# A decode kernel's last three microseconds: result in 16 rows of 144 columns, other weight pieces, and one early read

## Chip, cores, metric

The program uses one core of a Trainium2 chip (trn2). Runs of different rounds were on different chips, so each ratio is taken against the kernel before of the same rounds. The metric is the device time of the program in microseconds (us). The profiled span is about 1.8 us shorter than the device time (before: 210.4 against 212.2). The engines are PE (TensorE), DVE (VectorE), ACT (ScalarE), POOL (GpSimd) and SP (SyncE, which issues the DMAs here).

## The reference, cut to what matters

```python
# B = 4 batch rows, D = 576; 32 query heads, 16 KV heads of 128; a window of 2048 keys; F = 4608
xn  = layernorm(x)
A   = attention(xn @ wq, k_cache[last 2048], v_cache[last 2048]) @ wo
h   = gelu(layernorm(xn) @ w1) ...          # one token: all shifted parts are zero, so x1 = xn
Bm  = xn + gelu(layernorm(xn) @ w3) @ w4    # w4: 4608 x 576
out = x + A + Bm                            # 4 x 576, bf16
```

The K and V windows and the weights are read once, 87 MB. The result is 4.6 KB.

## The kernel before

All of `x + xn + A + gelu(..) @ w4` is summed in PSUM by PE. The result has 4 rows of 576 columns; the sum is kept as 8 rows of 288: row (batch, half). To aim a half at its row, the stationary operand is shifted by one column inside a tile that is zero elsewhere.

```python
CW = D // 2                                   # 288 columns
W4_PIECES = [0, 10, NFH, NFH + 10, NFH + 14, NF - 2, NF]      # NF = 36, NFH = 18: 10, 8, 10, 4, 2, 2 rows

OR = 2 * B                                    # 8 rows of the sum
OW = OR + 2
gT = cleared([P, NF, OW], "gT")               # activations, every second column, else zero
acc = ps_acc.tile([P, CW], F32)

def acc_matmuls(terms):
    for i in range(2):
        for n, (lhsT, rhs) in enumerate(terms):
            to, q, start = (second[0], QD, second[1]) if second and n % 2 else (acc, 0, False)
            nc.tensor.matmul(out=to[q:q + OR, :], lhsT=lhsT[:, 1 - i:1 - i + OR],
                             rhs=rhs[:, i * CW:(i + 1) * CW], start=start, stop=False, ...)
# ... (attention over 16 KV heads, the MLP's first product: cut)
mlp_out(*pieces[0])            # rows 0-9 of w4, odd rows into a second sum, acc_odd, in other PE columns
o_turn(hl); o_sum(hl); o_spread(hl); o_pick(hl)       # last attention head
mlp_out(*pieces[1])
o_proj(hl)
mlp_out(*pieces[2])
mlp_out(*pieces[3])
second.clear()                 # from here on all rows go into acc, one after the other
odd = const.tile([OR, CW], F32)
nc.scalar.activation(out=odd[:], in_=acc_odd[QD:QD + OR, :], func=ACT.Copy)
for lo, hi in pieces[4:]:
    mlp_out(lo, hi)
fin = const.tile([OR, CW], out.dtype)
nc.vector.tensor_tensor(out=fin[:], in0=acc[0:OR, :], in1=odd[:], op=ALU.add)
nc.sync.dma_start(out=o2.rearrange("b (i n) -> (b i) n", i=2), in_=fin[:])
```

While `second` is set, a pair of rows of w4 goes to two groups of PE columns at once, so a pair takes the time of one matmul. A "piece" is one DMA of w4; its landing releases PE for its rows. One "row" of w4 here is one of 36 slices of 128 x 576 in SBUF.

Of the kernel before, what the change touches and what calls it, by code (L numbers as in the profile page):

```python
# [9 lines left out]
ALU = mybir.AluOpType  # L10
AX = mybir.AxisListType
BF16 = mybir.dt.bfloat16
F32 = mybir.dt.float32
# [9 lines left out]
def kernel(  # L23
# [14 lines left out]
    nc = tc.nc  # L38
    P = 128
    B, Sq, D = A_x.shape  # L40
# [8 lines left out]
    NF = F // P  # L49
    NFH = NF // 2  # L50
# [4 lines left out]
    NQD = P // QD  # L55
    NSL = 4
    SC = NC // NSL
    CW = D // 2
    NW = SC * QD
    assert NW == 512 and NSL * NJ == QD and NQ == 2 * NQD * NW and NFH == 18  # L60
    scale = float(Dh) ** -0.5
# [5 lines left out]
    o2 = out.flatten_outer_dims()  # L67
# [14 lines left out]
    const = ctx.enter_context(tc.tile_pool(name="const", bufs=1))  # L82
# [47 lines left out]
        nc.sync.dma_start(out=t[:, KJ * F:], in_=B_w3[KJ * P:D, :].rearrange("r (e f) -> (r e) f", e=2))  # L130
        w_tiles["w3"] = t

    W4_PIECES = [0, 10, NFH, NFH + 10, NFH + 14, NF - 2, NF]

    def load_w4():
        t = wp.tile([P, NF, D], BF16, tag="w", name="w4_sb")
        for lo, hi in zip(W4_PIECES, W4_PIECES[1:]):
            e = lo // NFH
# [8 lines left out]
    ident_f = ident_w[:, 0:P]  # L147
# [7 lines left out]
    def cleared(shape, name):  # L155
        t = const.tile(shape, BF16, name=name)
        flat = t[:] if len(shape) == 2 else t[:].rearrange("p a b -> p (a b)")
        flat = flat.bitcast(F32)
        nc.scalar.activation(out=flat, in_=zero[:].bitcast(F32).to_broadcast(list(flat.shape)), func=ACT.Copy)
        return t  # L160
# [2 lines left out]
    ln2T = cleared([P, KJ + 2, QD], "ln2T")  # L163
    ZP = (NSL - 1) * NJ
    qz = cleared([P, ZP + Hkv * 4 * P], "qz")
    OR = 2 * B
    OW = OR + 2
    gT = cleared([P, NF, OW], "gT")
    op = cleared([P, WOR, OW], "op")

    acc = ps_acc.tile([P, CW], F32)
    nc.vector.memset(acc[:], 0.0)
# [2 lines left out]
    second = []  # L175

    def acc_matmuls(terms):
        for i in range(2):
            for n, (lhsT, rhs) in enumerate(terms):
                to, q, start = (second[0], QD, second[1]) if second and n % 2 else (acc, 0, False)  # L180
                nc.tensor.matmul(out=to[q:q + OR, :], lhsT=lhsT[:, 1 - i:1 - i + OR],  # L181
                                 rhs=rhs[:, i * CW:(i + 1) * CW], start=start, stop=False, skip_group_check=True)
                if start:
                    second[1] = False
# [43 lines left out]
    for kb in range(NQD):  # L228
        nc.vector.tensor_copy(out=sel[:, :, :, kb, :],
                              in_=ident_bf[:].rearrange("p (ib i e) -> p ib e i", ib=2, e=2))  # L230
# [19 lines left out]
    with nc.allow_low_precision("zeros and ones"):  # L250
# [7 lines left out]
                          in_=sel_j[:].unsqueeze(1).to_broadcast([P, NG, NJ]))  # L258
# [7 lines left out]

    idz = const.tile([B, OW], F32)
    nc.gpsimd.memset(idz[:], 0.0)
    nc.gpsimd.tensor_copy(out=idz[:, 1:OR + 1:2], in_=ident_f[0:B, 0:B])
    xsum = xn_f  # L270
    nc.vector.tensor_tensor(out=xsum[:], in0=xn_f[:], in1=x_bf[:], op=ALU.add)
    acc_matmuls([(idz[:], xsum)])
    ln2_bf = part(D, B)
    layernorm(None, ln2_bf, xn_bf)
# [25 lines left out]
    for r in range(2):  # L300
        nc.vector.tensor_copy(out=q_bf[:, r],
                              in_=qT_ps[:, r].rearrange("p u (g x) -> p g u x", g=NQD)[:, :, :, 0:B])
# [101 lines left out]
    def o_sum(h):  # L404
        oT = st.pop(("oT", h))
        v = oT[:].rearrange("p s (g x) -> p (s g) x", g=NQD)[:, :, 0:NJ].rearrange("p g (b r) -> p b r g", r=rep)
        k = h % WOQ
        if k == 0:
            st["on"] = small.tile([P, WOH, B], BF16, tag="on", name="on")
        with nc.allow_low_precision("summed in float32"):  # L410
            nc.vector.reduce_sum(out=st["on"][:, k * rep:(k + 1) * rep, :].rearrange("p r b -> p b r"),  # L411
                                 in_=v, axis=AX.X)
# [12 lines left out]
    def o_pick(h):  # L425
        if h % WOQ < WOQ - 1:
            return
        R = st.pop("R")
        mk = small.tile([P, WOR, WOH, B], BF16, tag="mk")
        nc.vector.tensor_tensor(out=mk[:], in0=R[:],  # L430
                                in1=own[:].unsqueeze(1).unsqueeze(3).to_broadcast([P, WOR, WOH, B]), op=ALU.mult)
        with nc.allow_low_precision("one term is not zero"):
            nc.vector.reduce_sum(out=op[:, :, 1:OR + 1:2], in_=mk[:].rearrange("p i h b -> p i b h"), axis=AX.X)

    def o_proj(h):
        if h % WOQ < WOQ - 1:
            return
        for i in range(0, WOR, 2):
            acc_matmuls([(op[:, i + u, :], wo_tiles[h // WOQ][:, i + u, :]) for u in range(2)])

    G_CHUNKS = [(e, 4 * g, 4) for e in range(2) for g in range(NQD)] + [(e, 16, 2) for e in range(2)]
    xs = const.tile([P, NF, B], F32, name="g_x")
# [31 lines left out]
    def mlp_act():  # L474
        u = const.tile([P, NF, B], F32, name="g_u")
        nc.vector.tensor_tensor(out=u[:], in0=xs[:], in1=xs[:], op=ALU.mult)
        nc.vector.tensor_scalar(out=u[:], in0=u[:], scalar1=GELU_A, scalar2=1.0, op0=ALU.mult, op1=ALU.add)
        nc.vector.tensor_tensor(out=u[:], in0=u[:], in1=xs[:], op=ALU.mult)
        nc.scalar.activation(out=u[:], in_=u[:], func=ACT.Tanh, scale=GELU_C)
        nc.vector.tensor_scalar(out=u[:], in0=u[:], scalar1=0.5, scalar2=0.5, op0=ALU.mult, op1=ALU.add)  # L480
        nc.vector.tensor_tensor(out=gT[:, :, 1:OR + 1:2], in0=u[:], in1=xs[:], op=ALU.mult)

    def mlp_out(lo, hi):
        w4 = w_tiles["w4"]
        for i in range(lo, hi, 2):
            acc_matmuls([(gT[:, i + u, :], w4[:, i + u, :]) for u in range(2)])


    order = [("K", 0), ("K", 1), ("K", 2)]
# [24 lines left out]
    for t in range(Hkv):  # L514
        hm, hv, hf, hp = t - 1, t - 2, t - 3, t - 4
        for s in range(NSL):
            if s == NSL - 1 and hm >= 0:
                sm_turn(hm)
            n = t * NSL + s + 1
# [3 lines left out]
            if s == 0:  # L523
                if hm >= 0:
                    sm_max(hm)
                if hv >= 0:
                    sm_rec(hv)
                if hp >= 0:
                    o_pick(hp)
                if hf >= 0:  # L530
                    o_scale(hf)
                k_mask(t)
            elif s == 1 and hm >= 0:
                sm_maxT(hm)
            elif s == 2:
                if hm >= 0:
                    sm_sub(hm)
                    sm_exp(hm)
                if hf >= 0:
                    o_sum(hf)  # L540
            elif s == 3 and hm >= 0:
                sm_den(hm)
# [12 lines left out]
            if t == G_AT:  # L555
                if s < 3:
                    mlp_g(s)
                if s > 0:
                    mlp_turn(s - 1)
                if s == NSL - 1:  # L560
                    mlp_act()
# [27 lines left out]
    o_sum(hl - 1)  # L589
    pieces = list(zip(W4_PIECES, W4_PIECES[1:]))  # L590
    acc_odd = ps_acc.tile([P, CW], F32, tag="g", name="acc_odd")
    second += [acc_odd, True]
    mlp_out(*pieces[0])
    o_turn(hl)
    o_sum(hl)
    o_spread(hl)
    o_pick(hl)
# [4 lines that stand above are left out]
    second.clear()  # L602
    odd = const.tile([OR, CW], F32)
    nc.scalar.activation(out=odd[:], in_=acc_odd[QD:QD + OR, :], func=ACT.Copy)
    for lo, hi in pieces[4:]:
        mlp_out(lo, hi)

    fin = const.tile([OR, CW], out.dtype)
    nc.vector.tensor_tensor(out=fin[:], in0=acc[0:OR, :], in1=odd[:], op=ALU.add)
    nc.sync.dma_start(out=o2.rearrange("b (i n) -> (b i) n", i=2), in_=fin[:])  # L610


# [28 lines left out]
```

## Time and profile before

| | before |
|---|---|
| device time, median of 3 | 212.24 us (212.07 to 212.55) |
| span of the profiled run | 210.4 us |
| DMA queue q1 | 87.17 MB, 97.4% of 16 engines' span |
| PE busy | 71% |
| last piece of w4 seen by PE | 207.09 us |

From the page of the kernel before: first the DMA row of 40 slices (tenths busy) and the bandwidth, then the DMA queues (packets, MB, share), then the chain that ended last, by engine.

```profile
DMA  7999999999999999999999999999999999999991
...
q1 hardware_dynamic: 6640, 87.17, 97.4%
q8 instruction: 7, 0.11, 0.2%
...
DMA 69%; PE 19%; DVE 8%; issue 1%; ACT 1%; SPq 0%; DVEq 0%
```

The DMA engines are at least 90% busy from the second slice to the 39th. Shortening work under this load is not expected to shorten the kernel, unless it moves fewer bytes or lets a transfer start sooner. What is left is the tail after the last weights.

The tail, from the timeline of the kernel before (start us, duration us, engine, line, operation, count; in brackets the engine's idle time before it and what ended that):

```profile
204.27 0.28 PE L181 MATMUL acc<-w_sb,gT 128*8 128x288 bf16 x1 [1.17 <-DMA w_sb<-in_B_w_dram]
...
206.35 0.40 ACT L604 ACTIVATE odd<-acc_odd 8x288 f32<-8x288 f32 x1 [7.80 <-PE acc_odd L181]
206.39 1.35 PE L181 MATMUL acc<-w_sb,gT 128*8 128x288 bf16 x8
206.39 0.45 PEld L181 LDWEIGHTS <-gT 128*8 128x8 bf16 x4 [0.28 <-issue]
207.09 0.33 PEld L181 LDWEIGHTS <-gT 128*8 128x8 bf16 x3 [0.25 <-issue]
207.85 0.45 DVE L609 TENSOR_TENSOR fin<-acc,odd 8x288 bf16<-8x288 f32 x1 [5.95 <-PE acc L181]
208.32 0.37 SPq L610 DMA_DIRECT2D out_dram<-fin  x1
```

And the end of the chain of waits of the kernel before (start us, us, what):

```profile
184.90 22.15 DMA w_sb<-in_B_w_dram
207.05 0.04 issue
207.09 0.67 PE acc L181 x4
207.75 0.03 issue
207.78 0.02 DVEq L609
207.80 0.04 issue
207.85 0.45 DVE fin L609
```

Here PE waits for DMA: the weight loads (PEld) stand idle 0.25 us before the last piece, and the chain goes from the DMA to the last four matmuls. Between them and the final add stands `DVEq L609`, a semaphore wait of its own on DVE: the add has to wait for PE and for ACT, and one of the two waits became a separate instruction. After the page's chain come the result's DMA, and SP's closing waits, which are not counted as busy. In the trace's records the last of these waits is passed at 209.59, 1.27 us after the result's DMA instruction starts; the program's close then takes 0.83 us.

### The profile page before, as it was taken

How to read it: one execution, taken by the hardware profiler on the slowest of the kernel's cores; microseconds unless marked ns; L12 is line 12 of the kernel's file. 1: busy time of each engine (PE TensorE's matmuls, PEld its weight loads, DVE VectorE, ACT ScalarE, POOL GpSimd, SP SyncE). 2: the span in 40 equal slices, each digit the busy share in tenths (PEclk: the TensorE clock that was granted, in tenths of full speed). 3: DMA queues.
4: the chain of work that ended last, by engine and by line, in shares of the span. 5: the costliest groups of instructions: out<-in, count | busy, mean ns of one | idle time of the engine just before them, and what ended most of it. 6: DMA issues, size and time to landing. Idle time of an engine off the chain costs nothing.

```text
span 210.4 us, 2389 instructions
## 1 busy us (share of the span) xinstructions
PE 149.7 (71%) x941; PEld 63.7 (30%) x955; DVE 120.3 (57%) x216; ACT 33.9 (16%) x64; POOL 2.8 (1%) x15
## 2 busy tenths in 40 slices
PE   0396595769691008649899599977995976888974
PEld 0132232123240003214364144333532321443542
DVE  4831989474850082825806878985399274683220
ACT  7603101020210000202102121120111020202300
POOL 4010000000000000000000000000000000000000
PEclk9999579796997555957999969997998596999999
DMA  7999999999999999999999999999999999999991
GB/s 281 417 399 436 424 437 419 434 436 424 440 441 411 439 420 426 440 436 420 439 430 420 439 421 436 427 436 431 420 438 430 424 432 433 424 433 425 427 400 52
DMA packets 6659, 87.32 MB, mean 415 GB/s; under 512 B 748, under 2 KB 760, under 8 KB 1400
## 3 DMA queue, kind: packets, MB, share of 16 engines
q1 hardware_dynamic: 6640, 87.17, 97.4%
q8 instruction: 7, 0.11, 0.2%
q14 instruction: 4, 0.03, 0.0%
q10 hardware_dynamic: 8, 0.00, 0.0%
HBM read 87.17 MB, written 0.00 MB: 414 GB/s over the span
## 4 chain that ended last, share of the span: by engine, by line
DMA 69%; PE 19%; DVE 8%; issue 1%; ACT 1%; SPq 0%; DVEq 0%
DMA vn<-in_A_v_cache_dram 37%; DMA w_sb<-in_B_w_dram 27%; PE S L336 7%; DMA wq_sb<-in_A_wq_dram 6%; DVE kt L223 4%; PE acc L181 2%; PE g_ps L454 2%; PE O L388 2%; PE q_ps L283 2%; PE oT L401 1%; DVE mx L342 1%; PE S L358 1%; DVE qz L315 1%; PE gT_ps L466 1%; PE qT_ps L298 0%
## 5 line engine op out<-in xcount | busy, mean ns | idle before, releaser
L223 DVE STREAM_TRANSPOSE kt<-kn 128x1024 int32<-128x1024 int32 x64 | 76.5, 1216 | 12.7 <-DMA kn<-in_A_k_cache_dram 11.9
L336 PE MATMUL S<-kt,qz 128*128 128x512 bf16 x242 | 76.8, 440 | 5.0 <-DVE kt L223 3.1
L388 PE MATMUL O<-vn,PT 128*32 128x512 bf16 x256 | 27.2, 424 | 37.7 <-DMA vn<-in_A_v_cache_dram 32.5
L336 PEld LDWEIGHTS <-qz 128*128 128x128 bf16 x256 | 21.8, 104 | 41.8 <-issue 26.5
L364 ACT ACTIVATE E<-S 128x512 bf16<-128x512 f32 x16 | 9.5, 597 | 121.9 <-PE S L358 121.9
L388 PEld LDWEIGHTS <-PT 128*32 128x32 bf16 x256 | 7.2, 94 | 46.2 <-issue 21.4
L370 DVE STREAM_TRANSPOSE PT<-E 128x512 bf16<-128x512 bf16 x16 | 11.4, 710 | 16.0 <-ACT E L364 15.9
L395 ACT ACTIVATE O_sb<-O,rd 128x512 f32<-128x512 f32 x16 | 11.0, 686 | 16.0 <-issue 11.0
L354 DVE TENSOR_REDUCE nm<-mg 8x1 bf16<-8x16 f32 x16 | 2.4, 149 | 17.4 <-PE mg L349 17.4
L411 DVE TENSOR_REDUCE on<-oT 128x8 bf16<-128x128 f32 x16 | 4.5, 280 | 13.7 <-PE oT L401 13.7
L401 PE MATMUL oT<-ident_w,O_sb 128*128 128x128 f32 x64 | 11.8, 316 | 0.1
L342 DVE TENSOR_REDUCE mx<-S 128x1 f32<-128x512 f32 x16 | 10.5, 657 | 1.3 <-PE S L336 1.3
L401 PEld LDWEIGHTS oT<-ident_w,O_sb 128*128 128x128 f32 x64 | 9.6, 166 | 5.1 <-issue 3.4
L181 PE MATMUL acc<-wo_sb,op 128*8 128x288 bf16 x56 | 7.7, 290 | 0.0
L358 PE MATMUL S<-nm,j_row 8*128 8x512 bf16 x16 | 6.8, 424 | 0.0
L181 PE MATMUL acc<-w_sb,gT 128*8 128x288 bf16 x40 | 5.9, 285 | 1.3 <-DMA w_sb<-in_B_w_dram 1.2
L374 PEld LDWEIGHTS dn<-rs,same_j 128*128 128x128 f32 x32 | 5.8, 188 | 2.9 <-ACT E L364 0.7
L327 PE MATMUL S<-negbig,ohT 4*128 4x512 bf16 x16 | 6.2, 385 | 0.2 <-issue 0.2
L349 PE MATMUL mg<-dm,sel_jb 128*8 128x16 bf16 x16 | 2.8, 174 | 3.9 <-DVE dm L344 3.5
L181 PEld LDWEIGHTS <-op 128*8 128x8 bf16 x64 | 4.6, 88 | 2.6 <-issue 0.7
L472 DVE COPY g_x<-gT_ps 128x64 f32<-128x64 f32 (+1 forms) x3 | 0.6, 194 | 7.7 <-PE gT_ps L466 7.7
L349 PEld LDWEIGHTS <-sel_jb 128*8 128x8 bf16 x16 | 1.3, 83 | 12.0 <-issue 5.4
(92 smaller groups left out, 85.1 us busy)
## 6 DMA issues: line engine op xcount, KB each, us to landing
kn<-in_A_k_cache_dram SPq DMA_DIRECT2D x16, 2048.0 KB, 22.2
vn<-in_A_v_cache_dram SPq DMA_DIRECT2D x16, 2048.0 KB, 24.6
wo_sb<-in_A_wo_dram SPq DMA_DIRECT2D x4, 1152.0 KB, 24.8
w_sb<-in_B_w_dram SPq DMA_DIRECT2D x1, 4608.0 KB, 34.7
wq_sb<-in_A_wq_dram SPq DMA_DIRECT2D x1, 4096.0 KB, 12.3
w_sb<-in_B_w_dram SPq DMA_DIRECT2D x2, 1440.0 KB, 29.2
w_sb<-in_B_w_dram SPq DMA_DIRECT2D x2, 576.0 KB, 32.9
w_sb<-in_B_w_dram SPq DMA_DIRECT2D x1, 1152.0 KB, 28.8
```

The source lines that it names most:

```text
L181: nc.tensor.matmul(out=to[q:q + OR, :], lhsT=lhsT[:, 1 - i:1 - i + OR], rhs=rhs[:, i * CW:(i + 1) * CW], start=start, stop=False, skip_gro ...
L223: nc.vector.transpose(out=kt[:], in_=src)
L327: nc.tensor.matmul(out=S_ps[h][:].rearrange("p (c k) -> p c k", k=QD), lhsT=ohT[:], rhs=negbig[:].unsqueeze(1).to_broadcast([B, SC, QD]), ...
L336: nc.tensor.matmul(out=S_ps[h][:], lhsT=qz[:, z0:z0 + P], rhs=kt[:, ib, :, e:2 * QD:2].rearrange("p c k -> p (c k)"), start=False, stop=Fa ...
L342: nc.vector.reduce_max(out=mx[:], in_=S_ps[h][:], axis=AX.X)
L358: nc.tensor.matmul(out=S_ps[h][:], lhsT=j_row[:], rhs=st.pop(("nm", h))[:, 0:1].to_broadcast([NJ, NW]), start=False, stop=False, skip_grou ...
L364: nc.scalar.activation(out=E[h][:].rearrange("p c k -> p (c k)"), in_=S_ps.pop(h)[:], func=ACT.Exp, scale=scale, accum_out=rs[:])
L370: nc.vector.transpose(out=PT[h][:], in_=E.pop(h)[:])
L374: nc.tensor.matmul(out=dn[:], lhsT=same_j[:], rhs=st.pop(("rs", h))[:], start=True, stop=True)
L388: nc.tensor.matmul(out=O_ps[h][g * QD:(g + 1) * QD], lhsT=PT[h][:, c, :], rhs=vn[:, :, c, :], start=(s == 0), stop=False, skip_group_check ...
L395: nc.scalar.activation(out=O_sb[h][:], in_=O_ps.pop(h)[:], func=ACT.Copy, scale=st.pop(("rd", h))[:, 0:1])
L401: nc.tensor.transpose(out=oT[:, s, :], in_=o[:, s, :], identity=ident_w[:, s * NJ:s * NJ + P])
```

## The change

The intent is to shorten the work after the last landing. Half the columns per row make the final add and the copy of the odd sum (`acc_odd`) shorter. The last pieces hold one row each, so that little is left when the last one lands. A one-element read of the odd sum makes DVE see ACT's semaphore early, and takes that wait off the final add.

```diff
--- before.py
+++ after.py
@@ -55,7 +55,8 @@
     NQD = P // QD
     NSL = 4
     SC = NC // NSL
-    CW = D // 2
+    NI = 4
+    CW = D // NI
     NW = SC * QD
     assert NW == 512 and NSL * NJ == QD and NQ == 2 * NQD * NW and NFH == 18
     scale = float(Dh) ** -0.5
@@ -130,7 +131,7 @@
         nc.sync.dma_start(out=t[:, KJ * F:], in_=B_w3[KJ * P:D, :].rearrange("r (e f) -> (r e) f", e=2))
         w_tiles["w3"] = t
 
-    W4_PIECES = [0, 10, NFH, NFH + 10, NFH + 14, NF - 2, NF]
+    W4_PIECES = [0, 10, NFH, NF - 6, NF - 2, NF - 1, NF]
 
     def load_w4():
         t = wp.tile([P, NF, D], BF16, tag="w", name="w4_sb")
@@ -163,8 +164,9 @@
     ln2T = cleared([P, KJ + 2, QD], "ln2T")
     ZP = (NSL - 1) * NJ
     qz = cleared([P, ZP + Hkv * 4 * P], "qz")
-    OR = 2 * B
-    OW = OR + 2
+    OR = NI * B
+    OW = OR + NI
+    ROWS = slice(NI - 1, NI - 1 + OR, NI)
     gT = cleared([P, NF, OW], "gT")
     op = cleared([P, WOR, OW], "op")
 
@@ -175,10 +177,10 @@
     second = []
 
     def acc_matmuls(terms):
-        for i in range(2):
+        for i in range(NI):
             for n, (lhsT, rhs) in enumerate(terms):
                 to, q, start = (second[0], QD, second[1]) if second and n % 2 else (acc, 0, False)
-                nc.tensor.matmul(out=to[q:q + OR, :], lhsT=lhsT[:, 1 - i:1 - i + OR],
+                nc.tensor.matmul(out=to[q:q + OR, :], lhsT=lhsT[:, NI - 1 - i:NI - 1 - i + OR],
                                  rhs=rhs[:, i * CW:(i + 1) * CW], start=start, stop=False, skip_group_check=True)
                 if start:
                     second[1] = False
@@ -266,7 +268,7 @@
 
     idz = const.tile([B, OW], F32)
     nc.gpsimd.memset(idz[:], 0.0)
-    nc.gpsimd.tensor_copy(out=idz[:, 1:OR + 1:2], in_=ident_f[0:B, 0:B])
+    nc.gpsimd.tensor_copy(out=idz[:, ROWS], in_=ident_f[0:B, 0:B])
     xsum = xn_f
     nc.vector.tensor_tensor(out=xsum[:], in0=xn_f[:], in1=x_bf[:], op=ALU.add)
     acc_matmuls([(idz[:], xsum)])
@@ -430,7 +432,7 @@
         nc.vector.tensor_tensor(out=mk[:], in0=R[:],
                                 in1=own[:].unsqueeze(1).unsqueeze(3).to_broadcast([P, WOR, WOH, B]), op=ALU.mult)
         with nc.allow_low_precision("one term is not zero"):
-            nc.vector.reduce_sum(out=op[:, :, 1:OR + 1:2], in_=mk[:].rearrange("p i h b -> p i b h"), axis=AX.X)
+            nc.vector.reduce_sum(out=op[:, :, ROWS], in_=mk[:].rearrange("p i h b -> p i b h"), axis=AX.X)
 
     def o_proj(h):
         if h % WOQ < WOQ - 1:
@@ -478,12 +480,12 @@
         nc.vector.tensor_tensor(out=u[:], in0=u[:], in1=xs[:], op=ALU.mult)
         nc.scalar.activation(out=u[:], in_=u[:], func=ACT.Tanh, scale=GELU_C)
         nc.vector.tensor_scalar(out=u[:], in0=u[:], scalar1=0.5, scalar2=0.5, op0=ALU.mult, op1=ALU.add)
-        nc.vector.tensor_tensor(out=gT[:, :, 1:OR + 1:2], in0=u[:], in1=xs[:], op=ALU.mult)
+        nc.vector.tensor_tensor(out=gT[:, :, ROWS], in0=u[:], in1=xs[:], op=ALU.mult)
 
     def mlp_out(lo, hi):
         w4 = w_tiles["w4"]
         for i in range(lo, hi, 2):
-            acc_matmuls([(gT[:, i + u, :], w4[:, i + u, :]) for u in range(2)])
+            acc_matmuls([(gT[:, u, :], w4[:, u, :]) for u in range(i, min(i + 2, hi))])
 
 
     order = [("K", 0), ("K", 1), ("K", 2)]
@@ -602,12 +604,14 @@
     second.clear()
     odd = const.tile([OR, CW], F32)
     nc.scalar.activation(out=odd[:], in_=acc_odd[QD:QD + OR, :], func=ACT.Copy)
+    seen = const.tile([1, 1], F32)
+    nc.vector.tensor_copy(out=seen[:], in_=odd[0:1, 0:1])
     for lo, hi in pieces[4:]:
         mlp_out(lo, hi)
 
     fin = const.tile([OR, CW], out.dtype)
     nc.vector.tensor_tensor(out=fin[:], in0=acc[0:OR, :], in1=odd[:], op=ALU.add)
-    nc.sync.dma_start(out=o2.rearrange("b (i n) -> (b i) n", i=2), in_=fin[:])
+    nc.sync.dma_start(out=o2.rearrange("b (i n) -> (b i) n", i=NI), in_=fin[:])
 
 
 # ---- launch: one core; inputs and outputs as the reference has them ----
```

## The prediction

> **What bounds it now.** DMA. In the page's slices DMA reads 9 in 38 of 40; one queue holds 97.4% of 16 engines' span; 87.17 MB come in at 414 GB/s; DMA is 69% of the chain of waits. PE is busy 71% but mostly waits for data. The change moves the same bytes in as many packets, so only what follows the last weight pieces can get shorter.
>
> **The tail before** (timeline; span 210.4 us). w4's last pieces release PE at 204.27 (10 rows), 205.65 (4), 206.39 (2) and 207.09 (2). The last four matmuls, of 288 columns, start 121 ns apart and end at 207.74. VectorE passes a separate semaphore wait, starts the final add at 207.85 and takes 0.446 us. The result's DMA is issued at 208.32, its wait passed at 209.59; closing takes 0.83 us.
>
> **What changes, costed.**
> 1. Twice as many matmuls of half the width. The Trainium skill ("TensorE: Matmul & The Clock Gate", "Wait — 56ns, not 53.3ns?") gives N/2.4 GHz + about 2.5 ns between warm starts: 122.5 ns for 288 columns, and the trace shows 121 to 122. For 144 that is 62.5 ns (estimate from that page). The doubled weight loads should stay hidden: the spread's matmuls, each with its own 128-column load, start 25 ns apart here. PE's total hardly changes.
> 2. The third piece's 12 rows land about 0.7 us later, near 204.97 (two rows cost 0.70 us between the last landings). Its 48 matmuls in concurrent pairs need 24 x 62 ns, to 206.46. The next 4 rows take PE to 206.96, the two single rows (8 x 62 ns, landed by 206.75 and 207.09) to a last start near 207.40. So PE, not the landing, is last by 0.1 us. The last matmul takes about 226 ns instead of 286: PE ends near 207.63: **0.11 us saved**. Caught up, it would be 0.24.
> 3. The odd sum's ACTIVATE falls from 0.40 to about 0.24 us, but starts later, near 207.17; the one-element read ends near 207.55, just before PE. It takes the separate wait off the final add: **0.06 us saved**.
> 4. Final add, 144 columns: 0.446 to about 0.30 us at 1 ns per column (the 512-column reduction takes 0.657): **0.15 us saved**.
> 5. Result DMA: 16 rows of 288 bytes on 16 engines for 8 of 576 on 8. Packets took 31 to 52 ns; issue to wait passed, 1.27 us, should stay within 0.1. The skill ("DMA: Bandwidth & Descriptors", Specifications) says that below 512 bytes a read-modify-write is done: a small loss is possible; no run yet shows it.
> 6. Larger clears on ScalarE and narrower fp32 matmuls early hide behind the wq load, which ends at 13.0.
>
> **Sum**: about 0.3 us saved, all on the critical path, 0.15% of the whole, against a spread of 0.48 us among the runs of before.
>
> **Predicted**: 211.95 us, 8 in 10 between 211.5 and 212.4. Faster by over 2%: 0.01; within 2%: 0.98; slower by over 2%: 0.01.
>
> **What would show it.** Matmuls about 62 ns apart; PE without idle time from the third piece on; final add 0.30 us, no separate wait; last landing still about 207.1; span about 210.1.
>
> **What would make it wrong.** Loads not hidden (spacing above 65 ns): 0.3 us or more lost; a result DMA landing later for its short rows; a throttled PE clock after the longer idle gap before the third piece (202.9 to 205.0); a shift in when buffers come free in the main loop, some tenths either way.

## The result, and the profile after

The changed kernel took 212.14 us (median of 6, 211.94 to 212.23) against 212.29 us (median of 6, 212.07 to 212.55). The ratio is 0.9991, 95% interval 0.9978 to 1.0003. Ratios are computed as the mean time of one kernel's runs over that of the other's of the same rounds, so they are not quite the ratio of the medians. The interval contains 1: by the total alone the two kernels are the same, and what the change did has to be read from the tail.

The same parts of the page, changed kernel:

```profile
DMA  7999999999999999999999999999999999999991
...
q1 hardware_dynamic: 6656, 87.17, 97.5%
q8 instruction: 8, 0.13, 0.2%
...
DMA 65%; PE 22%; DVE 8%; issue 1%; SPq 1%; ACT 1%; DVEq 0%
```

The same bytes move. The 16 additional packets of q1 are 8 result rows more and 8 completion writes more. There is one more packet on q8, which the page calls "instruction"; it comes up again below.

The tail in the timeline of the changed kernel:

```profile
205.00 0.22 PE L183 MATMUL acc<-w_sb,gT 128*16 128x144 bf16 x1 [1.73 <-DMA w_sb<-in_B_w_dram]
205.00 2.46 PEld L183 LDWEIGHTS <-gT 128*16 128x16 bf16 x71 [1.87 <-issue]
205.01 0.23 PE L183 MATMUL acc_odd<-w_sb,gT 128*16 128x144 bf16 x1
205.06 0.22 PE L183 MATMUL acc<-w_sb,gT 128*16 128x144 bf16 x1
...
207.00 0.66 PE L183 MATMUL acc<-w_sb,gT 128*16 128x144 bf16 x8
207.21 0.28 ACT L606 ACTIVATE odd<-acc_odd 16x144 f32<-16x144 f32 x1 [8.56 <-PE acc_odd L183]
207.52 0.14 DVE L608 COPY seen<-odd 1x1 f32<-1x1 f32 x1 [5.47 <-ACT odd L606]
207.70 0.30 DVE L613 TENSOR_TENSOR fin<-acc,odd 16x144 bf16<-16x144 f32 x1
208.03 0.36 SPq L614 DMA_DIRECT2D out_dram<-fin  x1
```

And the end of its chain of waits:

```profile
207.11 0.05 PE acc L183
207.17 0.50 PE acc L183 x8
207.68 0.02 issue
207.70 0.30 DVE fin L613
```

71 weight loads run in one stretch from 205.00 without idle time: PE no longer waits for the last landings, it is behind: the last piece's last completion is recorded at 207.13, and the first matmul of its row starts at 207.25. So the chain now stays on PE back to 205.00, where the third piece released it. The separate wait of DVE is gone, and the add takes 0.30 us.

When the last packet lands varies by some tenths from profile to profile, so the tail is best counted from there. The table holds, for each profile told in this text, in us: the end of the last weight packet, its completion write included (from the trace's DMA records; time from the span's start), and from there on the stretches, one after the other, to the end of the span.

| kernel | last weight packet ends at | to PE's end | to the add | add | to DMA instruction | to SP's last closing wait | close | sum after the packet |
|---|---|---|---|---|---|---|---|---|
| before | 206.73 | 1.01 | 0.11 | 0.45 | 0.03 | 1.27 | 0.83 | 3.69 |
| changed | 206.81 | 0.86 | 0.04 | 0.30 | 0.03 | 1.38 | 0.83 | 3.43 |
| changed, again | 206.97 | 0.86 | 0.04 | 0.30 | 0.03 | 1.38 | 0.83 | 3.43 |
| pieces alone | 206.72 | 0.85 | 0.11 | 0.45 | 0.03 | 1.27 | 0.83 | 3.52 |
| columns alone | 206.78 | 1.02 | 0.11 | 0.30 | 0.03 | 1.38 | 0.83 | 3.66 |
| read alone | 206.83 | 1.00 | 0.04 | 0.45 | 0.03 | 1.27 | 0.83 | 3.61 |
| 8 engines, 288 bytes | 206.61 | 0.97 | 0.11 | 0.45 | 0.03 | 1.95 | 0.84 | 4.34 |
| 16 engines, 144 bytes | 207.00 | 0.87 | 0.04 | 0.30 | 0.03 | 1.87 | 0.83 | 3.93 |
| seven pieces, 144 columns | 207.12 | 0.76 | 0.04 | 0.30 | 0.03 | 1.53 | 0.83 | 3.49 |
| seven pieces, 288 columns | 206.59 | 0.76 | 0.04 | 0.45 | 0.03 | 1.39 | 0.83 | 3.49 |
| fetch early | 206.58 | 1.00 | 0.11 | 0.45 | 0.03 | 1.27 | 0.83 | 3.68 |
| fetch late | 206.66 | 1.00 | 0.11 | 0.45 | 0.03 | 1.28 | 0.83 | 3.69 |
| extra piece | 206.86 | 1.00 | 0.11 | 0.45 | 0.03 | 1.31 | 0.83 | 3.71 |
| last slot, 288 columns | 206.67 | 0.73 | 0.04 | 0.45 | 0.03 | 1.27 | 0.83 | 3.33 |

Where kernels have the same columns and pieces, the time to PE's end repeats within 0.04 us, and where a later stretch has the same form, it repeats within about 0.01, so differences can be read here that no total shows. (The profile models the end of a matmul, but records the start of the add: the sum of the two columns before the add doesn't depend on the model. It falls from 1.12 to 0.90.) The change saves 0.26 us after the last packet: 0.15 to PE's end, 0.07 before the add, 0.15 in the add, less 0.11 lost between the result's DMA instruction and the last wait. The total showed 0.15 us.

In the kernels in which PE is behind (changed, changed again, pieces alone, 16 engines), the last packet isn't what releases PE's last work. There PE's end comes 2.66 us (pieces alone: 2.61) after the first matmul of the third piece. Counting from the last packet still compares them, because it ends 1.76 to 1.80 us after that matmul in all four.

### The profile page after: what moved, and what is told of

It is laid out like the page before. It is cut to its first block, busy times and chain, and to the rows that moved or that the text cites. A ratio compares the mean times of both kernels' runs of the same rounds, so it can differ in the third digit from the quotient of the medians.

```text
span 210.2 us, 2668 instructions
## 1 busy us (share of the span) xinstructions
PE 147.8 (70%) x1080; PEld 66.8 (32%) x1095; DVE 120.2 (57%) x217; ACT 34.0 (16%) x64; POOL 2.8 (1%) x15
## 3 DMA queue, kind: packets, MB, share of 16 engines
q1 hardware_dynamic: 6656, 87.17, 97.5%
HBM read 87.17 MB, written 0.00 MB: 415 GB/s over the span
## 4 chain that ended last, share of the span: by engine, by line
DMA 65%; PE 22%; DVE 8%; issue 1%; SPq 1%; ACT 1%; DVEq 0%
DMA w_sb<-in_B_w_dram 33%; DMA vn<-in_A_v_cache_dram 27%; PE S L338 9%; DMA wq_sb<-in_A_wq_dram 6%; DVE kt L225 4%; PE O L390 3%; PE g_ps L456 2%; PE acc L183 2%; PE q_ps L285 2%; PE oT L403 1%; DVE mx L344 1%; PE S L360 1%; DVE qz L317 1%; PE gT_ps L468 1%; ACT q_sb L296 1%
## 5 line engine op out<-in xcount | busy, mean ns | idle before, releaser
L403 PE MATMUL oT<-ident_w,O_sb 128*128 128x128 f32 x64 | 10.6, 292 | 0.0
L403 PEld LDWEIGHTS oT<-ident_w,O_sb 128*128 128x128 f32 x64 | 8.7, 154 | 4.5 <-issue 2.2
L183 PE MATMUL acc<-wo_sb,op 128*16 128x144 bf16 x112 | 7.7, 226 | 0.0
L183 PEld LDWEIGHTS <-op 128*16 128x16 bf16 x128 | 6.9, 90 | 0.6 <-issue 0.3
L183 PE MATMUL acc<-w_sb,gT 128*16 128x144 bf16 x76 | 5.2, 226 | 1.7 <-DMA w_sb<-in_B_w_dram 1.7
L183 PEld LDWEIGHTS <-gT 128*16 128x16 bf16 x144 | 4.8, 90 | 2.1 <-issue 2.0
```

The source lines that it names most:

```text
L183: nc.tensor.matmul(out=to[q:q + OR, :], lhsT=lhsT[:, NI - 1 - i:NI - 1 - i + OR], rhs=rhs[:, i * CW:(i + 1) * CW], start=start, stop=False ...
L403: nc.tensor.transpose(out=oT[:, s, :], in_=o[:, s, :], identity=ident_w[:, s * NJ:s * NJ + P])
```

## The experiments

Four questions were open. Which part of the change moved PE's end? Why does the result's transfer take 0.11 us longer? Where did the rest go, from 0.26 us in the tail to 0.15 in the total? And is there a better version?

Theory A is the sum of tail terms as predicted, with PE's end moved by the pieces. Rival B says the longer result transfer was chance; rival C says that the narrower columns brought PE's end forward.

### Control: the changed kernel again

No edit; the changed kernel again.

> The changed kernel once more, unaltered, as a control. Theory A (the tail terms are real and repeat; about 0.1 us of the gain was lost in the result's transfer because it now has 16 short rows): last matmul end to start of the final add about 0.04 us, final add 0.30 us, start of the result's DMA instruction to the passing of its wait again 1.33 to 1.43 us (1.38 in the first profile; 1.27 before). Theory B (the 1.38 against 1.27 us was chance of one profile): this interval comes out between 1.2 and 1.3 us this time. Total: 0.1 to 0.3 us under before.

Measured: 212.12 us against 212.25 (5 and 9 runs), ratio 0.9992 (0.9979 to 1.0004). The result's transfer is 1.38 us again and the tail 3.43 us again. Rival B falls. The last packet ended at 206.97, 0.17 us later than in the first profile: that is the noise in which the total's gain stands.

### Pieces alone

```diff
-    W4_PIECES = [0, 10, NFH, NFH + 10, NFH + 14, NF - 2, NF]
+    W4_PIECES = [0, 10, NFH, NF - 6, NF - 2, NF - 1, NF]
-            acc_matmuls([(gT[:, i + u, :], w4[:, i + u, :]) for u in range(2)])
+            acc_matmuls([(gT[:, u, :], w4[:, u, :]) for u in range(i, min(i + 2, hi))])
```

> Only the pieces of w4 (10, 8, 12, 4, 1, 1 rows), still 288 columns and 8 rows of result, no early read. Theory A (PE's end is moved by the pieces, not by narrower matmuls): the third piece frees PE near 205.0 us; 12 pairs at 122 ns, 4 pairs, then 4 single matmuls at 121 ns; the last starts near 207.32 and ends near 207.60, so 0.14 us before that of the kernel before (207.74), and even a little before that of the changed kernel (207.66). Rival C (the narrower columns brought the earlier PE end): PE ends near 207.74 as before. The rest of the tail as before: separate wait, add 0.45 us, result transfer 1.27 us under theory A of the result rows. Total about 0.14 us under before.

Measured: 212.05 us, ratio 0.9993 (0.9981 to 1.0006). Timeline of this run:

```profile
206.91 0.65 PE L181 MATMUL acc<-w_sb,gT 128*8 128x288 bf16 x4
...
207.12 0.40 ACT L604 ACTIVATE odd<-acc_odd 8x288 f32<-8x288 f32 x1 [8.58 <-PE acc_odd L181]
207.68 0.45 DVE L609 TENSOR_TENSOR fin<-acc,odd 8x288 bf16<-8x288 f32 x1 [5.77 <-PE acc L181]
```

The four matmuls of the two single rows end at 207.57, 0.85 us after the last packet. The kernel before needed 1.01, the changed one 0.86. So the pieces alone give all of the gain at PE's end, with 288 columns.

### Columns alone

The changed kernel with the old pieces and without the early read:

```diff
-    W4_PIECES = [0, 10, NFH, NF - 6, NF - 2, NF - 1, NF]
+    W4_PIECES = [0, 10, NFH, NFH + 10, NFH + 14, NF - 2, NF]
-    seen = const.tile([1, 1], F32)
-    nc.vector.tensor_copy(out=seen[:], in_=odd[0:1, 0:1])
```

> Only the 16 rows of 144 columns; pieces as before (10, 8, 10, 4, 2, 2), no early read. Theory A: 8 matmuls of 144 columns follow the last landing (near 207.09), 62.5 ns apart, last start 207.53, end 207.75: PE ends as before, nothing gained there (rival C: about 0.1 us earlier). Separate semaphore wait of VectorE still there, 0.10 us from PE's end to the add; final add 0.30 us (0.15 saved); result transfer about 1.38 us (0.1 lost). Total within 0.1 us of before.

Measured: 212.35 us, ratio 1.0002 (0.9990 to 1.0015). Timeline of this run:

```profile
206.68 1.12 PE L183 MATMUL acc<-w_sb,gT 128*16 128x144 bf16 x12
...
207.91 0.30 DVE L611 TENSOR_TENSOR fin<-acc,odd 16x144 bf16<-16x144 f32 x1 [5.87 <-PE acc L183]
208.23 0.36 SPq L612 DMA_DIRECT2D out_dram<-fin  x1
```

PE ends 1.02 us after the last packet, as before (1.01): rival C falls. The add gains 0.15 us, the transfer loses 0.11. The narrow rows are worth about 0.03 us together (sums 3.69 and 3.66).

### Read alone

```diff
     nc.scalar.activation(out=odd[:], in_=acc_odd[QD:QD + OR, :], func=ACT.Copy)
+    seen = const.tile([1, 1], F32)
+    nc.vector.tensor_copy(out=seen[:], in_=odd[0:1, 0:1])
```

> Only the early one-element read of the odd sum, else the kernel before. Theory A: VectorE's separate semaphore wait ahead of the final add is gone, and from the last matmul's end to the add 0.04 us instead of 0.11; all else as before, result transfer 1.27 us; 0.06 us saved. Rival: the gap is that of PE's semaphore reaching VectorE and stays at 0.1 us, the read is worth nothing.

Measured: 212.25 us, ratio 0.9999 (0.9985 to 1.0013). Timeline of this run:

```profile
206.89 0.14 DVE L606 COPY seen<-odd 1x1 f32<-1x1 f32 x1 [4.90 <-ACT odd L604]
...
207.87 0.45 DVE L611 TENSOR_TENSOR fin<-acc,odd 8x288 bf16<-8x288 f32 x1 [0.83 <-PE acc L181]
```

The separate wait is gone, and from PE's end to the add it is 0.036 us instead of 0.108. So the read is worth 0.07 us in the tail. The single parts add up: pieces 0.17, columns 0.03, read 0.08, together 0.28 (counted on sums after the packet), against 0.26 measured for all three.

### Why 16 result rows land later

Theory D: the number of DMA engines that get a share costs (8 or 16, counted by the completion writes in the records). Theory E: the number or shortness of the writes costs. The first run cuts the 8 rows of the kernel before in two (16 writes, 8 engines); the second does the same to the changed kernel (32 writes, 16 engines).

```diff
-    fin = const.tile([OR, CW], out.dtype)
+    fin_w = const.tile([OR, 2, CW // 2 + 8], out.dtype)
+    fin = fin_w[:, :, 0:CW // 2]
-    nc.sync.dma_start(out=o2.rearrange("b (i n) -> (b i) n", i=2), in_=fin[:])
+    nc.sync.dma_start(out=o2.rearrange("b (i u n) -> (b i) u n", i=2, u=2), in_=fin)
```

> The kernel before, but its 8 result rows are cut in two in the tile (8 columns of padding between), so the result goes out as 16 writes of 288 bytes on 8 engines. Tells apart why 16 rows took 1.38 us from the DMA instruction's start to the passed wait, and 8 rows 1.27 us, in three profiles each. Theory D (the number of engines that get a share costs): stays near 1.27 us. Theory E (number or shortness of the writes costs): near 1.38 us. All before the transfer is as in the kernel before (final add within 0.03 us of 0.446).

> The changed kernel, its 16 result rows cut in two: 32 writes of 144 bytes on 16 engines. Theory D (engines cost): still near 1.38 us. Theory E (number or shortness of the writes): longer again, by about 0.1 to 0.2 us, 1.5 to 1.6 us. The rest as in the changed kernel.

Measured: 212.78 us (ratio 1.0028, 1.0012 to 1.0043) and 212.48 us (1.0014, 1.0001 to 1.0028). Both were slower than either theory said, mostly for a reason that neither had: the DMA instruction itself. In the timelines:

```profile
208.16 0.88 SPq L612 DMA_DIRECT2D out_dram<-fin_w  x1
```

```profile
208.24 0.68 SPq L616 DMA_DIRECT2D out_dram<-fin_w  x1
```

It took 0.88 and 0.68 us instead of 0.37 and 0.36. From the DMA records of these and the first runs, in us:

| | writes, engines | instruction | its end to first write | first write to last completion write | to the passed wait |
|---|---|---|---|---|---|
| before | 8 x 576 B, 8 | 0.372 | 0.419 | 0.115 | 0.366 |
| changed | 16 x 288 B, 16 | 0.360 | 0.502 | 0.164 | 0.354 |
| 8 engines, 288 bytes | 16 x 288 B, 8 | 0.876 | 0.598 | 0.112 | 0.366 |
| 16 engines, 144 bytes | 32 x 144 B, 16 | 0.682 | 0.656 | 0.169 | 0.364 |

The spread from the first write to the last goes with the engines and not with the number or size of the writes (0.11 for 8 engines, 0.16 to 0.17 for 16; the tile's rows are 8 and 16 in the same runs, so engines and rows aren't told apart). It is 0.05 of the lost 0.11 us. The delay before the first write (0.08 longer in the changed kernel) also grew where only the cut of the rows changed, so theories D and E can't be told apart for this part: the cut also changed the DMA's access pattern. What is excluded is a slower completion of short writes: from the last completion write to the passed wait it is 0.35 to 0.37 us in all four. The Trainium skill ("DMA: Bandwidth & Descriptors", Specifications) says that below 512 bytes a read-modify-write is done. No run here shows a cost of it.

### Seven pieces

In the changed kernel PE is behind at the last landing. With pieces of 10, 8, 10, 4, 2, 1 and 1 rows, it should have caught up.

```diff
-    W4_PIECES = [0, 10, NFH, NF - 6, NF - 2, NF - 1, NF]
+    W4_PIECES = [0, 10, NFH, NFH + 10, NFH + 14, NF - 2, NF - 1, NF]
     mlp_out(*pieces[3])
+    mlp_out(*pieces[4])
     second.clear()
-    for lo, hi in pieces[4:]:
+    for lo, hi in pieces[5:]:
```

The second of these runs is the same on 288 columns and 8 result rows, with the early read.

> The changed kernel with seven pieces (10, 8, 10, 4, 2, 1, 1 rows; the odd sum takes in the piece of two), so that PE has caught up when the last row lands. Theory A: PE waits for the last landing near 207.1 us, its last four matmuls start 62.5 ns apart, PE ends 0.41 us after that landing is seen (207.5) instead of 207.66; gap to the add 0.04, add 0.30, transfer 1.38. Total 0.3 to 0.4 us under before, 0.1 to 0.2 under the changed kernel. Rival: the additional DMA delays the landings by as much as PE gains.

> The same seven pieces and the early read, with 288 columns and 8 result rows. Theory A: after the last landing two matmuls of 288 columns, 121 ns apart, PE ends 0.41 us after the landing is seen, as in the run with 144 columns; gap 0.04 us, add 0.45, transfer 1.27. So the columns are worth only the add minus the transfer: this ends 0.03 to 0.06 us later than the run with 144 columns, counted from the last landing. Total 0.25 to 0.35 us under before.

Measured: 212.19 us (ratio 0.9997, 0.9984 to 1.0009) and 212.06 us (0.9990, 0.9977 to 1.0002), so the expected totals were missed, by at least 0.3 and 0.13 us. PE behaved as expected: its end comes 0.41 us after the first matmul that the last landing released, and 0.76 us after the last packet, in both. But the closing waits gave it back: 1.53 instead of 1.38 us, and 1.39 instead of 1.27. SP's instructions at the close of the 288-column run, from the trace's records (start us, ns, semaphores waited for; the result's DMA now counts on S100):

```
207.858 362  DMA_DIRECT2D  out_dram<-fin   (completion: S100)
208.271  28  wait S106, S105
208.341  28  wait S107, S102
208.819 302  wait S108, S100
209.183  28  wait S109, S101
209.252  28  wait S110, S103
```

The wait for the result ends at 209.12, 1.26 us after the DMA instruction, just as before. But two more waits follow it and cost 0.13 us. In the kernel before the result's DMA counted on S110, which SP waits for last. With one DMA more, it got another semaphore of the rotation.

The 144-column run has another miss: its last packet ended at 207.12, the latest of all. The rival, that the additional DMA delays the landings, doesn't explain it: the 288-column run has the same seven pieces, and its last packet ended at 206.59.

### Is it the additional DMA?

```diff
-    W4_PIECES = [0, 10, NFH, NFH + 10, NFH + 14, NF - 2, NF]
+    W4_PIECES = [0, 4, 10, NFH, NFH + 10, NFH + 14, NF - 2, NF]     # and mlp_out by the shifted indices
```

> The kernel before with its first w4 piece cut in two (4 and 6 rows), so one DMA more ahead of the result's. Theory H (the closing instructions of SyncE wait for the DMA semaphores in a fixed order; with one DMA more the result's gets a semaphore that is waited for in the middle, and two further waits then follow it): the time from the result's DMA instruction to the last of those waits grows from 1.27 to about 1.40 us, and the last write itself still ends 0.90 us after the instruction's start. Rival: the seven-piece runs were longer there for their single rows; then 1.27 us here.

Measured: 212.32 us, ratio 1.0006 (0.9993 to 1.0020). The last write ends 0.90 us after the instruction's start, as expected. The closing stretch is 1.31 us, longer than 1.27 but less than the 1.40 expected. The records say why: here S100 is paired with S109, its wait passes 1.27 us after the DMA instruction, and only one wait follows, 0.04 us. So theory H holds in kind: not being last cost 0.04 us here and 0.13 us there, by what still followed. Its size was wrong because the pairing of the waits differs from kernel to kernel.

### Is it an instruction fetch?

The page shows one more packet of q8 in the changed kernel. In the trace these are 16 KB packets, with 197 to 327 recorded PE instructions from one to the next in the changed kernel, 267 on average (some records are missing from a trace). In the changed kernel one falls at 204.67 and takes 0.94 us, beside the last weights; in the kernel before the last falls at 200.34. All four profiles of 16-row kernels with single-row pieces had one between 204.3 and 205.0, and their last packets ended late: 206.81, 206.97, 207.00 and 207.12, against 206.59 to 206.83 in the other profiles taken by then (one of which, columns alone with 206.78, had such a fetch too). Theory F made the fetch the cause. To test it, tiny matmuls into unread PSUM rows shift the fetches of the kernel before:

```diff
+            if s == 0 and 2 <= t < 6:
+                for _ in range(18):          # 32 in the control
+                    nc.tensor.matmul(out=acc[64:96, 0:4], lhsT=ident_bf[:, 0:32], rhs=ident_bf[:, 0:4],
+                                     start=False, stop=False, skip_group_check=True)
```

> The kernel before with 128 tiny matmuls (each with its weight load, so 256 PE instructions) early in the main loop, into rows of the accumulator that nobody reads. Control for the next run. Theory F (an instruction fetch of 16 KB for PE, once every 256 of its instructions, shares a DMA engine with the last weights; the doubled matmuls of the changed kernel bring one near 204.6 us, which makes the last landing later): here there is one more fetch, but early; the late ones stay where they were in the kernel before (last near 200.3 us), so the end of the last weight packet stays within 206.5 to 206.85 us and the total within 0.1 us of before.

> The kernel before with 72 such tiny matmuls (144 PE instructions), which shifts the fetches so that one should fall near 204 to 205 us, as in the changed kernel, with columns, pieces and tail of the kernel before. Theory F: the last weight packet ends near 206.9 us (five profiles with such a fetch so far: 206.78 to 207.12; five without: 206.59 to 206.83), the total is 0.1 to 0.3 us above before. Rival G (the later landings of the changed kernels come from their single-row pieces or from chance): ends by 206.85 us, total as before.

Measured: the control took 212.07 us (ratio 0.9999, 0.9986 to 1.0012), the other 212.21 us (1.0003, 0.9990 to 1.0017). The fetch did fall at 204.33 in the second run, as built (the control's last one fell at 201.80, not near 200.3 as expected). Its last packet nevertheless ended at 206.66, against 206.58 in the control. Theory F falls as it was put: a late fetch alone did not delay the last packet here.

The landing records tell more. Each weight DMA has 16 completions. In the three profiles with the latest last packets (changed again, 16 engines, seven pieces on 144 columns) fifteen completions of the last piece are in by 206.88 to 207.01, no later than in the other profiles (206.85 to 207.09), and one comes 0.26, 0.45 and 0.42 us after them. One completion already lags in the same three in the DMA that lands near 170.5, by 0.24, 0.52 and 0.47 us. So what made those landings late was there 34 us before the fetch and before any piece of w4 landed: neither the late fetch nor the single-row pieces began it. Single rows on 288 columns also ended early, 206.59 to 206.72 in three kernels. Such a lag can be made up: pieces alone had 0.24 near 170 us and 0.02 at the end. Why one completion lags, and whether a late fetch can keep it from catching up, is not shown. In the last piece it lags by 0.12 us or more in all five profiles with 144 columns, and by 0.05 at most in eight of the nine with 288 (extra piece: 0.17). With one profile each this is a hint, no more, that narrow rows cost something before the tail. The totals leave room for about 0.1 us: 0.26 us gained after the last packet, 0.15 and 0.13 in the medians.

### A version to beat both

If the narrow rows are worth next to nothing, 288 columns are kept, with six pieces again, so that the result's DMA keeps the last place. The first two pieces become one of 18 rows, and the last head's work moves ahead of it.

```diff
-    W4_PIECES = [0, 10, NFH, NFH + 10, NFH + 14, NF - 2, NF]
+    W4_PIECES = [0, NFH, NFH + 10, NFH + 14, NF - 2, NF - 1, NF]
-    mlp_out(*pieces[0])
     o_turn(hl); o_sum(hl); o_spread(hl); o_pick(hl)      # cut: four lines
-    mlp_out(*pieces[1])
+    mlp_out(*pieces[0])
     o_proj(hl)
-    mlp_out(*pieces[2])
-    mlp_out(*pieces[3])
+    for lo, hi in pieces[1:4]:
+        mlp_out(lo, hi)
     second.clear()
     # cut: the odd sum's copy
+    seen = const.tile([1, 1], F32)
+    nc.vector.tensor_copy(out=seen[:], in_=odd[0:1, 0:1])
```

(and the loop over single rows of the change.)

> A kernel to beat both: 288 columns and 8 result rows, w4 in six pieces of 18, 10, 4, 2, 1 and 1 rows (so the result's DMA keeps the last place among the closing waits, PE is caught up at the last row, and no further instruction fetch comes), the final output head's spread ahead of the first piece, early read of the odd sum. From the end of the last weight packet to the end of the span: before 3.69 us, changed kernel 3.43; here PE ends about 0.76 us after that packet (1.01 before), add after 0.04 more, 0.45, issue 0.03, 1.27, 0.83: 3.37 us. Total 0.25 to 0.4 us under before. Rival: the single piece of 18 rows leaves PE behind, and its end is not before 207.7 us.

Measured: 211.89 us (211.78 to 212.00, 5 runs) against 212.19 us (9 runs of before), 0.30 us less as expected; ratio 0.9985, 95% interval 0.9972 to 0.9997. It is the only one of the thirteen intervals told here that lies wholly below 1, and it does so by 0.0003, which chance could do once among so many; the stretches of its tail are the stronger evidence. Timeline of this run:

```profile
206.64 0.75 PE L181 MATMUL acc<-w_sb,gT 128*8 128x288 bf16 x4
206.72 0.40 ACT L603 ACTIVATE odd<-acc_odd 8x288 f32<-8x288 f32 x1 [7.56 <-PE acc_odd L181]
206.99 0.08 PEld L181 LDWEIGHTS <-gT 128*8 128x8 bf16 x1
207.15 0.14 DVE L605 COPY seen<-odd 1x1 f32<-1x1 f32 x1 [5.19 <-ACT odd L603]
207.43 0.45 DVE L610 TENSOR_TENSOR fin<-acc,odd 8x288 bf16<-8x288 f32 x1
207.90 0.36 SPq L611 DMA_DIRECT2D out_dram<-fin  x1
```

The last four matmuls straddle the last landing (206.99), PE ends 0.73 us after the last packet, and the tail is 3.33 us (3.37 expected), 0.36 less than before and 0.10 less than in the changed kernel. The rival, that the single piece of 18 rows leaves PE behind and its end not before 207.7, falls: PE ended at 207.39. It was not run against the changed kernel in the same rounds; over the kernel before of their own rounds the ratios are 0.9985 and 0.9992, and their intervals overlap.

## Why the prediction was right or wrong, point by point

The predicted time (211.95 us, range 211.5 to 212.4) holds the measured 212.14, and the change is within 2%, as it said. Neither proves much: the range also holds the 212.29 of the kernel before. About 0.3 us was predicted and 0.15 measured; the difference is smaller than the interval of the ratio (0.0025, about 0.5 us from end to end), so it is judged by the terms.

- **DMA bounds the kernel; only the tail can gain.** Right: the DMA row and 87.17 MB are the same after, the last packet ended no earlier (206.81 and 206.97 against 206.73), and the gain lies after it.
- **Matmuls 62.5 ns apart.** Right. They start 61 to 63 ns apart in the trace's records of one sum, weight loads hidden. The feared throttle did not come either: the granted clock was 1.00 from 203 to 208 us in both profiles.
- **PE falls behind and ends near 207.63.** Right in mechanism: third piece at 205.00 (predicted 204.97), the two single rows from 207.00, end at 207.66. Counted from the last packet the gain is 0.15 us, predicted 0.11. What the prediction did not say is that the pieces alone do this, and that half the columns do nothing for PE's end: it counted a shorter last matmul (226 for 286 ns), but columns alone gained nothing there (1.02 against 1.01). The Trainium skill ("TensorE: Matmul & The Clock Gate", Single matmul latency) gives (398 + N)/2.4 ns warm, so 286 and 226 ns for 288 and 144 columns; the traces have 286 and 226 too, but the profile models the ends of matmuls, so this is no independent check.
- **The odd sum and its read.** ACTIVATE 0.28 us for 0.24, read over at 207.67 for 207.55: level with PE's end instead of ahead of it, without harm. The saved wait: 0.07 us, predicted 0.06.
- **Final add 0.30 us.** Right: 0.296.
- **Result DMA "should stay within 0.1".** This is the term that was mis-sized: 0.11 us longer in three profiles of the 16-row form. The prediction looked for a loss in read-modify-writes; the runs show a later first write (0.08) and a wider spread over 16 engines (0.05), and an unchanged completion. Only the spread is traced to the engines or rows; the cause of the later first write is open.
- **Sum about 0.3.** 0.26 after the last packet. The rest, up to the measured total, lies in when the last packet lands. One of 16 completions lags there from long before the tail; the prediction named a shift in the main loop as a risk, but what shifted is not settled.
- **Early clears and matmuls hide behind the wq load.** Not tested by a run of its own. The first DMA issued after that load starts at 13.06 us before and 13.05 in the changed kernel.

## What to carry to other kernels

When a kernel is bound by DMA to the end, cut the last transfers so that the engine has caught up when the last one lands, and count the tail from the last packet, since the landing itself varies more than the gain (206.59 to 207.12 here, against 0.26 us). Look at a landing's completions one by one: a single late one of 16 can set it. Narrowing an operation on the last chain helps only by what the next link doesn't take back: here 0.15 us in the add against 0.11 in a transfer over twice as many rows. One more DMA anywhere can shift which semaphore the last one counts on, and what still follows that wait at the close.

## What the Trainium skill lacked or had wrong

- "TensorE: Matmul & The Clock Gate", Back-to-back issue gap, gives about 81 ns per matmul for a sustained stream of weight load and matmul at N = 128, and calls N/2.4 + 2.5 the isolated gap. Here a stream of weight loads (16 columns) and matmuls of 144 columns started 61 to 63 ns apart in one column group, with a second group beside it at the same pace, so N/2.4 + 2.5 (62.5) held for the stream, with these narrow loads. Eight matmuls of 32 columns, each with a weight load of 128 columns, started 25 ns apart.
- "DMA: Bandwidth & Descriptors" has no figure for what a small store costs by its shape. Here, from instruction to passed wait: 1.27 us for 8 rows of 576 bytes, 1.38 for 16 rows of 288; 1.95 for 8 rows cut in two and 1.87 for 16 rows cut in two, of which the DMA instruction alone took 0.88 and 0.68 us instead of 0.36 to 0.37.
- No page that was read for this tells of a cost by the order of the closing semaphore waits: 0.04 to 0.13 us here when the result's DMA isn't the last waited for.
